# The output transfers of a streaming recurrent-memory kernel, issued by GpSimd in place of SyncE

## The chip, the cores and the metric

The kernel runs on one core of a Trainium2 chip. The metric is device time in microseconds. It was timed in three runs before the change: 2551.04, 2555.86 and 2556.03 us, median 2555.86 us. The profile is one further execution under the hardware profiler, 2564.14 us on the device, whose span from the first to the last instruction is 2562.2 us.

In the text PE is the matrix engine (TensorE), DVE the vector engine, ACT the scalar engine, POOL is GpSimd and SP is SyncE. "SPq" and "ACTq" in a row of the profile are the instruction queues of SP and ACT that issue transfers. L248 means line 248 of the kernel.

## The reference

The input x has 2048 rows of 1024 numbers in bfloat16. It is layer-normalised to xn, and the output is x + A(xn) + B(xn).

A is attention with a recurrent memory. The rows are cut into 64 segments of 32 rows. To each segment 8 memory rows are joined in front, so 40 rows are projected to queries, keys and values of 32 heads with 128 numbers each, attended under a mask, and projected back to 1024 columns. The first 8 of the 40 result rows are the memory of the next segment, so the segments must run one after another:

```
for s in range(n_seg):
    h = concatenate([mem, x[:, s*32:(s+1)*32]])        # 40 rows
    q, k, v = h @ Wq, h @ Wk, h @ Wv                   # 1024 -> 32 x 128, each
    o = softmax(mask(q k^T * scale)) v @ Wo            # 32 x 128 -> 1024
    mem = o[:, :8];  outs.append(o[:, 8:])
```

B scores all rows, takes the best two, puts them through a gated network with 3584 hidden numbers, scales them and adds them back at their two rows. It is done once, ahead of the segments.

## The kernel before

**Weights.** Wq, Wk, Wv and Wo together are 64 granules, each 128 partitions x 2048 numbers, 512 KB. 42 granules stay in SBUF for the whole kernel. The other 22 are read from HBM again in each of the 64 segments, through 6 slots (`wstream`, tile name `g`). `fetch` (L236 to L249) issues the next such transfer on SP at L248. `used(g)` calls it when the program has come past a streamed granule, so each fetch goes into the slot of the granule just used and has to wait until PE is done with it. The streamed granules are spread evenly, about one in three: 1, 4, 7, 10, 13 and so on.

**A segment.** Segment s has the place j = s mod 4 in its group of four, G. Six phases of 8 granules project the segment's rows (L507 to L534, matmuls at L510): Wq, Wk for the first half of the heads, Wq, Wk for the second, Wv, Wv. Rows that do not depend on the memory ("left" rows, 8 of each segment, four segments together) ride along in some phases (L514): in segments with j = 1 and j = 2 their queries and keys are made and written to DRAM (`qkl_d<-QS`, 128 KB, issued by ACT, twice in such a segment). Then 16 granules of Wo (L549) make the result WO. ACT and DVE cast it into OB (L575, L576), PE transposes OB, and DVE puts the 8 memory rows into the ST of the next segment (L267). With j = 3 the left rows of the group are projected as well, into WL and then OL (L591).

**Hooks.** Work beside the matmuls is hung on (phase, granule in the phase) by `hook` and run in the program after that granule. What matters here:

- (0, 2) of the next segment: `store`, four transfers of OB to the output on SP (L579), 24 rows of 512 B each, 12 KB.
- (0, 5) of the segment after a group's last: `store_left`, four transfers of OL on SP (L596), 32 rows of 512 B each, 16 KB.
- (1, 4): ACT issues the load ZT (L394); (2, 3): ACT issues the load of the next ST (L260).
- (2, 5) and (4, 5): `scores`. It begins with a POOL copy of the left keys from QKL into KT (L432), without which the score matmuls (L436, L438) can't run. `scores(0)` also clears a part of PL on POOL (L456).
- (4, 6): `split_z`, a copy and a clear on POOL (L398, L399).

After the last segment both stores are run at once.

**Queues.** Each engine takes its instructions in the program's order, and one that waits holds what is behind it. SP's queue holds the weight fetches and the stores; ACT's holds its computing and the loads ZT, ST, QKL, STL and the writes `qkl_d<-QS`; POOL's holds only the small operations named above.

**Landing counters.** The library that builds the program tells the landing of a transfer by a semaphore. The transfers of SP and ACT, in one common order, take eight such counters in turn. Where a counter comes round again, the new transfer is made to wait until the earlier transfer with this counter, eight places before it in that order, has landed, whatever either of them carries. In the program before, the four stores and the four left stores take places in this order like any other. Around the store of a segment with j = 3 the order is: load ZT, two fetches, load ST, four stores, then the fetch that follows the use of granule 4. This fetch is the eighth place after ZT. GpSimd's transfers have eight counters of their own, and none was issued before.

Of the kernel before, what the change touches and what calls it, by code (L numbers as in the profile page):

```python
# [25 lines left out]
def kernel(  # L26
# [16 lines left out]
    nc = tc.nc  # L43
# [4 lines left out]
    SEG = int(A_seg_len)  # L48
# [8 lines left out]
    XM = SEG - M  # L57
# [4 lines left out]
    out2 = out[0]  # L62
# [267 lines left out]
    for c in range(2):  # L330
        nc.sync.dma_start(out=zT_d[bass.ds(vals[c] >> 5, 1), :, :, bass.ds(vals[c] & 31, 1)].rearrange("s p k r -> p (s k) r"),
                          in_=ZNEW[:, :, c:c + 1])
# [38 lines left out]
    for s in range(NSEG):  # L371
# [131 lines left out]
        for p, (mat, half) in enumerate(PHASES):  # L503
            PSm = psA.tile([P, 512], F32, tag="acc", name="PSm")
            PSl = psL.tile([P, 512], F32, tag="accl", name="PSl") if mat in left else None
            for kc in range(KC):
                g = 8 * p + kc  # L507
# [68 lines left out]
        nc.vector.tensor_copy(out=OB[:, P:256], in_=WO[:, P:256])  # L576
        def store(OB=OB, s=s):
            for g in range(4):
                nc.sync.dma_start(out=out2[s * SEG:s * SEG + XM, 256 * g:256 * (g + 1)],  # L579
                                  in_=OB[32 * g:32 * g + XM, :])  # L580

        todo = [store]
# [6 lines left out]
        if j == 3:  # L589
            OL = one.tile([P, 256], BF16, tag="pm", name="OL")  # L590
            nc.scalar.copy(out=OL[:, :], in_=WL[:, 0:256])  # L591

            def store_left(OL=OL, G=G):
                o4 = out2[4 * G * SEG:4 * (G + 1) * SEG, :].rearrange("(s r) d -> s r d", s=4)
                for g in range(4):
                    nc.sync.dma_start(out=o4[:, XM:SEG, 256 * g:256 * (g + 1)], in_=OL[32 * g:32 * (g + 1), :])  # L596
            todo.append(store_left)
        if s + 1 < NSEG:
            ST = nxt["st"]
# [37 lines left out]
```

## Time and profile before

| | |
|---|---|
| median of three runs (lowest, highest) | 2555.86 us (2551.04, 2556.03) |
| profiled execution: on the device, its span | 2564.14 us, 2562.2 us |
| PE busy | 1865.3 us, 73% of the span |
| DVE, ACT, POOL busy | 638.4, 513.5, 108.0 us |
| moved by the DMA engines | 831.71 MB, of it 800.19 MB on SP's queue |
| mean granted clock of PE | 0.883 |
| first store issued | 237.1 us after the span's start |
| transfers of OB and OL | 256 and 64 |

The page's slices show for each fortieth of the span how many tenths an engine was busy, and the mean share of the 16 DMA engines that had a packet in work. "DMA share" in a table by stretches is the same share; as it is summed from packets, it can come out a little over 1. "A <- B: t, n, m" in a table of waits means that A waited t us in n waits, the longest m, and that B ended them. The chain of waits goes back from the end, at each step to what released it.

### The profile page before, as it was taken

The numbers are of one execution on the slowest core, as the hardware profiler recorded it, in microseconds if no ns is written. First come the engines' busy times: TensorE is split into PE (matmuls) and PEld (weight loads), VectorE is DVE, ScalarE is ACT, GpSimd is POOL, SyncE is SP. The second block draws the span as 40 slices with busy tenths as digits, with TensorE's granted clock in tenths as the row PEclk, the third lists the DMA queues.
The fourth block names the chain that finished last, engine by engine and source line by source line (L and its number), as shares of the span: only waits on it lengthen the run. The fifth ranks groups of instructions, "written<-read, shape, count | busy, mean of one in ns | idle before, by whom it ended". The sixth has DMA issues, their size and how long they took to land.

```text
span 2562.2 us, 82489 instructions
## 1 busy us (share of the span) xinstructions
PE 1865.3 (73%) x36873; PEld 975.1 (38%) x36873; DVE 638.4 (25%) x1733; ACT 513.5 (20%) x1145; POOL 108.0 (4%) x371
## 2 busy tenths in 40 slices
PE   4366777777777777677777777777776877777676
PEld 3233343344334334333433343343333433343333
DVE  5302222222222222222222222222232222222222
ACT  4202122121212212111221212122121221122111
POOL 4200000000000000000000000000000000000000
PEclk9568989898989989988898988999899988889889
DMA  9997999999999989989998999999998998999898
GB/s 333 298 353 244 341 320 323 316 351 340 311 332 326 340 297 328 335 299 334 329 349 302 344 322 321 341 330 339 313 334 309 360 320 302 334 327 340 320 336 293
DMA packets 368855, 831.71 MB, mean 325 GB/s; under 512 B 69458, under 2 KB 122738, under 8 KB 368500
## 3 DMA queue, kind: packets, MB, share of 16 engines
q1 hardware_dynamic: 303668, 800.19, 87.3%
q10 hardware_dynamic: 64832, 26.25, 3.8%
q8 instruction: 288, 4.72, 0.7%
q14 instruction: 67, 0.55, 0.1%
HBM read 804.28 MB, written 22.02 MB: 322 GB/s over the span
## 4 chain that ended last, share of the span: by engine, by line
DMA 62%; PE 27%; issue 4%; DVE 3%; ACT 2%; SPq 2%; ACTq 1%; POOL 0%; DVEq 0%; POOLq 0%
DMA g<-in_A_Wv_dram 15%; DMA g<-in_A_Wq_dram 14%; DMA g<-in_A_Wo_dram 13%; PE PSm L510 12%; DMA g<-in_A_Wk_dram 6%; PE WO L549 4%; PE PSl L514 3%; DMA qkl_d<-QS 2%; DMA QKL<-qkl_d 2%; PE WL L549 2%; DMA ZT<-zT_d 2%; PE PTq L408 1%; DMA ST<-xT_d 1%; SPq L248 1%; DMA zT_d<-Tz 1%
## 5 line engine op out<-in xcount | busy, mean ns | idle before, releaser
L510 PE MATMUL PSm<-wres,ST 128*32 128x512 bf16 x8192 | 785.2, 423 | 15.7 <-DVE ST L267 13.6
L510 PE MATMUL PSm<-g,ST 128*32 128x512 bf16 x4096 | 450.9, 427 | 325.8 <-DMA g<-in_A_Wk_dram 136.0
L510 PEld LDWEIGHTS <-ST 128*32 128x32 bf16 x12288 | 329.0, 101 | 770.2 <-issue 413.8
L549 PEld LDWEIGHTS <-OT 128*32 128x32 bf16 x8192 | 224.8, 102 | 170.5 <-issue 150.9
L522 ACT CAST XB<-PSm 128x512 bf16<-128x512 f32 x256 | 150.2, 587 | 660.6 <-PE PSm L510 535.2
L549 PE MATMUL WO<-wres,OT 128*32 128x256 bf16 x5120 | 248.2, 293 | 17.3 <-issue 17.3
L549 PE MATMUL WO<-g,OT 128*32 128x256 bf16 x3072 | 169.1, 294 | 99.6 <-DMA g<-in_A_Wo_dram 83.8
L514 PE MATMUL PSl<-wres,STL 128*32 128x512 bf16 x2048 | 210.4, 398 | 2.7 <-DMA STL<-stl_d 2.7
L488 ACT CAST OT<-OP 128x256 bf16<-128x256 f32 x256 | 95.5, 373 | 324.6 <-PE OP L485 324.6
L448 ACT ACTIVATE SPS<-SPS 128x320 f32<-128x320 f32 x128 | 54.0, 422 | 528.4 <-DVE SPS L447 503.7
L416 DVE COPY KT<-PTq 128x512 bf16<-128x512 bf16 x128 | 54.4, 425 | 348.9 <-PE PTq L408 348.6
L408 PE MATMUL PTq<-IDENT,XB 128*128 128x128 bf16 x1024 | 112.9, 240 | 35.6 <-ACT XB L522 33.6
L446 DVE TENSOR_REDUCE NM<-SPS 128x8 f32<-128x320 f32 x128 | 63.0, 492 | 302.0 <-PE SPS L441 302.0
L432 POOL COPY KT<-QKL 128x128 bf16<-128x128 bf16 x128 | 37.3, 291 | 2335.4 <-PE WO L549 1057.4
L490 DVE CAST OTL<-OP 128x64 bf16<-128x64 f32 x128 | 28.8, 225 | 406.8 <-ACT OT L488 406.8
L408 PEld LDWEIGHTS <-XB 128*128 128x128 bf16 x1024 | 64.2, 104 | 166.2 <-ACT XB L522 131.5
L413 DVE COPY QT<-PTq 128x512 bf16<-128x512 bf16 x128 | 53.2, 416 | 261.1 <-PE PTq L408 261.0
L514 PEld LDWEIGHTS <-STL 128*32 128x32 bf16 x3072 | 86.3, 100 | 70.8 <-issue 14.0
L483 PE MATMUL OP<-PT,VM 32*128 32x40 bf16 x2048 | 94.9, 180 | 19.3 <-ACT VM L532 14.4
L514 PE MATMUL PSl<-g,STL 128*32 128x512 bf16 x1024 | 105.2, 397 | 0.0
L483 PEld LDWEIGHTS <-VM 32*128 32x128 bf16 x2048 | 66.2, 92 | 94.9 <-issue 58.7
L485 PE MATMUL OP<-PT,VL 32*128 32x40 bf16 x2048 | 88.1, 176 | 4.2 <-ACT VL L534 4.2
(99 smaller groups left out, 1513.4 us busy)
## 6 DMA issues: line engine op xcount, KB each, us to landing
g<-in_A_Wq_dram SPq DMA_DIRECT2D x384, 512.0 KB
g<-in_A_Wo_dram SPq DMA_DIRECT2D x384, 512.0 KB
g<-in_A_Wk_dram SPq DMA_DIRECT2D x320, 512.0 KB
g<-in_A_Wv_dram SPq DMA_DIRECT2D x320, 512.0 KB
qkl_d<-QS ACTq DMA_DIRECT2D x64, 128.0 KB
QKL<-qkl_d ACTq DMA_DIRECT2D x128, 64.0 KB
g<-in_B_w_gate_dram SPq DMA_DIRECT2D x16, 448.0 KB
g<-in_B_w_up_dram SPq DMA_DIRECT2D x16, 448.0 KB
```

The source lines that it names most:

```text
L408: nc.tensor.transpose(out=PTq[:, il, :, :].rearrange("p j r -> p (j r)"), in_=XB[:, il * P:(il + 1) * P], identity=IDENT[:, :])
L413: nc.vector.tensor_copy(out=QT[half][:, :, :], in_=pv)
L416: nc.vector.tensor_copy(out=KT[half][:, :, 0:32], in_=pv)
L446: nc.vector.tensor_reduce(out=NM[:, :], in_=S8, axis=AX.X, op=ALU.max, negate=True)
L448: nc.scalar.activation(out=S8, in_=S8, func=ACTF.Exp, scale=SCALE)
L483: nc.tensor.matmul(o, lhsT=VM[half][q0:q0 + 32, il * P:(il + 1) * P], rhs=PTm[q0:q0 + 32, il, 0:NK], start=True, stop=False, tile_position ...
L485: nc.tensor.matmul(o, lhsT=VL[q0:q0 + 32, c0:c0 + P], rhs=PTl[q0:q0 + 32, il, 0:NK], start=False, stop=True, tile_position=(q0, 0), skip_g ...
L488: nc.scalar.copy(out=OT[half][:, 2 * ph:2 * ph + 2, :, :], in_=ov[:, :, :, 0:SEG])
L510: nc.tensor.matmul(PSm[32 * jq:32 * jq + 32, :], lhsT=ST[:, kc, :], rhs=Gv[:, 512 * jq:512 * (jq + 1)], start=(kc == 0), stop=(kc == KC - ...
L514: nc.tensor.matmul(PSl[32 * jq:32 * jq + 32, :], lhsT=STL[:, kc, :], rhs=Gv[:, 512 * jq:512 * (jq + 1)], start=(kc == 0), stop=(kc == KC - 1),
L522: nc.scalar.copy(out=XB[:, :], in_=PSm[:, :])
L549: nc.tensor.matmul(PS[32 * g:32 * g + 32, 0:256], lhsT=lhs(h), rhs=Gv[:, D * hs + 256 * g:D * hs + 256 * (g + 1)], start=False, stop=(last ...
```

## The change

The two places where the output is written (L579 and L596) now name GpSimd as the issuing engine. Their data, shapes, order and place in the program stay.

```diff
         def store(OB=OB, s=s):
             for g in range(4):
-                nc.sync.dma_start(out=out2[s * SEG:s * SEG + XM, 256 * g:256 * (g + 1)],
+                nc.gpsimd.dma_start(out=out2[s * SEG:s * SEG + XM, 256 * g:256 * (g + 1)],
                                   in_=OB[32 * g:32 * g + XM, :])
...
             def store_left(OL=OL, G=G):
                 o4 = out2[4 * G * SEG:4 * (G + 1) * SEG, :].rearrange("(s r) d -> s r d", s=4)
                 for g in range(4):
-                    nc.sync.dma_start(out=o4[:, XM:SEG, 256 * g:256 * (g + 1)], in_=OL[32 * g:32 * (g + 1), :])
+                    nc.gpsimd.dma_start(out=o4[:, XM:SEG, 256 * g:256 * (g + 1)], in_=OL[32 * g:32 * (g + 1), :])
```

A transfer issued by GpSimd has its descriptors written by software on that engine; one issued by SyncE or ScalarE has them made by hardware.

## The prediction

> **What bounds the kernel now.** I read the page first, then the waits of PE, then the waits of SP, then the stretches behind the stores. The page (span, DMA slices, DMA queue of SP):
>
> ```profile
> span 2562.2 us, 82489 instructions
> ...
> DMA  9997999999999989989998999999998998999898
> ...
> q1 hardware_dynamic: 303668, 800.19, 87.3%
> ```
>
> SP's queue, nearly all of it weights, keeps the DMA engines busy for most of the time, but not for all of it. PE's two largest waits are for these weights, us in total, number, longest:
>
> ```profile
> PE PSm L510 <- DMA g<-in_A_Wk_dram: 136.0, 93, 5.7
> PE PSm L510 <- DMA g<-in_A_Wq_dram: 99.9, 109, 4.1
> ```
>
> So the streamed weights set the pace. The DMA share (the next to last number) says whether the stream itself is full. Here is the whole stretch of the segments, one 12 us stretch late in a segment, and then the 9 us that begin 3 us after the first store transfer of eight segments in a row, with j = 1, 2, 3, 0, 1, 2, 3, 0:
>
> ```profile
> 237.00:2555.00 2318.00, 1744.98 (x35222) 897.58 (x35218) 569.35 (x1571) 455.54 (x1050) 63.29 (x313) 0.90 0.92 328
> 1150.00:1162.00 12.00, 9.27 (x242) 5.45 (x241) 3.42 (x11) 3.58 (x10) 0.27 (x2) 0.94 1.05 390
> 1129.00:1138.00 9.00, 7.60 (x149) 3.34 (x141) 2.83 (x6) 2.37 (x5) 0.29 (x1) 1.00 0.72 217
> 1167.00:1176.00 9.00, 7.62 (x145) 3.41 (x138) 3.78 (x11) 2.18 (x4) 0.62 (x3) 1.00 0.90 283
> 1203.00:1212.00 9.00, 4.88 (x85) 1.75 (x80) 1.42 (x3) 0.59 (x1) 0.62 (x3) 0.85 0.72 230
> 1243.00:1252.00 9.00, 5.00 (x89) 1.70 (x81) 3.03 (x9) 1.60 (x3) 0.62 (x3) 0.72 0.69 211
> 1278.00:1287.00 9.00, 6.32 (x129) 2.90 (x121) 3.30 (x10) 2.18 (x4) 0.62 (x3) 1.00 0.87 263
> 1312.00:1321.00 9.00, 7.32 (x141) 3.35 (x133) 3.66 (x10) 2.18 (x4) 0.62 (x3) 1.00 0.84 266
> 1348.00:1357.00 9.00, 4.87 (x93) 1.86 (x85) 1.81 (x4) 0.59 (x1) 0.62 (x3) 0.95 0.70 216
> 1388.00:1397.00 9.00, 4.51 (x97) 2.04 (x95) 3.77 (x10) 1.60 (x3) 0.62 (x3) 1.00 0.48 140
> ```
>
> Late in a segment the DMA engines are full (1.05, 390 GB/s). Behind every store there is a hole. With j = 3 it is this one: SP issues four stores, then nothing until 1206.50; a slice of that time moves 0 GB/s; and the chain of waits leads into the fetch at 1206.50 from the load of ZT, which lands at 1201.29 + 5.14 = 1206.43:
>
> ```profile
> 1199.84 3.77 SPq L579 DMA_DIRECT2D out_dram<-OB  x4
> 1206.50 0.36 SPq L248 DMA_DIRECT2D g<-in_A_Wq_dram  x1
> ```
> ```profile
> 1206.00:1207.00 1.00, 0.77 (x12) 0.27 (x12) 0.06 (x1) 0.00 (x0) 0.00 (x0) 1.00 0.00 0
> ```
> ```profile
> 1201.29 5.14 DMA ZT<-zT_d
> ```
>
> The fetch does not read ZT. It has ZT's landing counter, because four stores stand between them. The same in SP's waits over the whole span: stores that wait for weights and ZT, which they do not touch, and fetches that wait for ZT and QS:
>
> ```profile
> SPq L248 <- DMA qkl_d<-QS: 174.6, 48, 8.8
> SPq L248 <- DMA ZT<-zT_d: 57.2, 26, 3.5
> SPq L579 <- DMA g<-in_A_Wk_dram: 66.3, 61, 3.5
> SPq L579 <- DMA g<-in_A_Wq_dram: 10.6, 19, 1.1
> SPq L596 <- DMA g<-in_A_Wq_dram: 18.1, 15, 2.3
> SPq L596 <- DMA ZT<-zT_d: 10.6, 7, 3.6
> ```
>
> **The change part by part.** *Taken from SP:* 320 issues, and with them four or eight places in the turn of eight counters. SP's own issue time is off the path, since SP mostly waits; what counts is that fetches no longer stand behind stores. With j = 3 the place eight after ZT then falls on a QKL load, and the fetches after granules 4, 7 and 10 have their slots free as soon as PE is done with them. Six slots stay in use, so I expect the hole gone there. With j = 0 the same holds for eight stores in place of four. With j = 1 and 2 the writes of QS still share counters with fetches (the 174.6 us stay as they are, no store stands between them), and I take half of these holes as gone.
>
> From the eight rows, 9 us times (1 - share): j = 1 and 2: 2.52 + 0.90 + 1.17 + 1.44 = 6.03 us; j = 3 and 0: 2.52 + 2.79 + 2.70 + 4.68 = 12.69 us. Gone: half of the first and all of the second, 15.7 us in eight segments, 1.96 us in one. 63 segments follow a store: **124 us**. The unknown is how much of a filled hole comes back elsewhere. From below: nothing is gained, if other transfers hold the fetches as long. From above: the DMA engines are never idle, 2318 us times (1 - 0.92) = 185 us. I take 124 because the holes at j = 3 and 0 end with a wait that the change removes, and the stretches without stores are full.
>
> By the Trainium skill (DMA: Bandwidth & Descriptors, section "Issuing engines are not separate DMA queues") transfers of all engines run on the same 16 DMA engines, and issuing from another engine saves only the issue time, usually small; by that sentence alone the 124 us would be 0, while the rows above show fetches held by landings and not by issue time.
>
> *Given to POOL:* the issue of 4 or 8 transfers, ahead of the copy L432 in its queue. No row has a software-made transfer. The nearest rows are SP's issues of the same transfers (min, median, max in ns) and, for the longest that POOL takes over one instruction, an addition in the prologue (mean 2118 ns):
>
> ```profile
> L579 SPq DMA_DIRECT2D out_dram<-OB x256: 302/352/1460, 237.1 to 2556.8; - x128
> L596 SPq DMA_DIRECT2D out_dram<-OL x64: 615/618/773, 352.2 to 2559.3; - x64
> L168 POOL TENSOR_TENSOR XP<-XP,XN 128x1024 bf16<-128x1024 bf16 x16 | 33.9, 2118 | 42.2 <-ACT XN L163 42.2
> ```
>
> I bound it by 0.35 and 2.12 us and take 1.0 us, nearer to SP's issues, since these are the same transfers, than to a long POOL computation. What is queued behind: L432 (0.29 us), and behind it the score matmuls. The sources of the stores, that copy, and PE around its need of it:
>
> ```profile
> 1197.89 0.29 DVE L576 CAST OB<-WO 128x128 bf16<-128x128 f32 x1 [2.07 <-DMA g<-in_A_Wq_dram]
> ...
> 1234.97 0.29 DVE L576 CAST OB<-WO 128x128 bf16<-128x128 f32 x1 [2.19 <-ACT OB L575]
> ```
> ```profile
> 1239.38 0.37 ACT L591 CAST OL<-WL 128x256 bf16<-128x256 f32 x1 [4.44 <-PE WL L549]
> ```
> ```profile
> 1197.68 0.29 POOL L432 COPY KT<-QKL 128x128 bf16<-128x128 bf16 x1 [24.40 <-PE WO L549]
> ```
> ```profile
> 1209.60 0.62 PE L510 MATMUL PSm<-g,ST 128*32 128x512 bf16 x4 [2.83 <-DMA g<-in_A_Wq_dram]
> 1209.98 0.27 PE L436 MATMUL SPS<-KT,QT 128*32 128x40 bf16 x4
> ```
> ```profile
> 1247.44 0.62 PE L510 MATMUL PSm<-g,ST 128*32 128x512 bf16 x4 [2.04 <-DMA g<-in_A_Wq_dram]
> 1247.82 0.27 PE L436 MATMUL SPS<-KT,QT 128*32 128x40 bf16 x4
> ```
>
> At 1.0 us: OB is ready at 1198.18, four issues end at 1202.2, L432 at 1202.5; needed at 1209.98, or without PE's stall of 2.83 us at 1207.1. Hidden by the phases 0 and 1, 4.6 us to spare. With j = 0: OL is ready at 1239.75, the OB issues are done by then, four more end at 1243.75, L432 at 1244.0; needed at 1247.82 - 2.04 = 1245.8, 1.8 us to spare. Cost 0. At 0.35 us also 0. At 2.12 us the ordinary segment still just fits (1206.9 against 1207.1); with j = 0, where OB is ready at 1235.26, eight issues and L432 end at 1235.26 + 16.96 + 0.29 = 1252.5, 6.7 us late, 15 times: 101 us. Stores that are held longer free OB and OL later, but OB is written again a segment later, and OL's buffer (that of PM) only after these scores.
>
> *The end:* the last stores have no cover. The sources and SP's last issues:
>
> ```profile
> 2554.22 0.29 DVE L576 CAST OB<-WO 128x128 bf16<-128x128 f32 x1 [2.19 <-ACT OB L575]
> ```
> ```profile
> 2556.37 0.37 ACT L591 CAST OL<-WL 128x256 bf16<-128x256 f32 x1 [2.18 <-PE WL L549]
> ```
> ```profile
> 2557.31 2.63 SPq L596 DMA_DIRECT2D out_dram<-OL  x4
> ```
>
> SP's last issue ends at 2559.94, and 2.26 us later the span ends. On POOL eight issues of 1.0 us from 2554.51 end at 2562.5, so **+2.6 us** (at 0.35 us -1.8, at 2.12 us +11.5).
>
> *Sum:* the profiled execution's 2564.1 - 124 + 2.6 = 2442.7 us. It lies 8.3 us over the median of the runs (2555.86), so for the median: **2434 us**.
>
> **The rivals.** *Half the gain* (A): the fetches meet the next landing in turn, QS, QKL or ST, and the holes move. For it: the 174.6 us behind QS and the holes of 0.90 and 0.84 where QS is written. Against it: only j = 1 and 2 write QS. 62 us less: 2496 us.
>
> *No change* (B): the holes come from the slots, not from the counters; SP would have waited for PE anyway, as it does elsewhere, and POOL's stores only save issue time. For it: in a stream with a fixed number of slots a late fetch often just follows a late PE. Against it: the chain goes through a landing at 1206.43, not through PE, and PE itself then waited 2.83 us for weights. 2556 us. This is also what the skill's sentence above gives.
>
> *Slower* (C): POOL's software descriptors take so long that L432 is late and PE waits at the scores, in each segment. With p us for an issue the ordinary segment is late by 4p - 8.7 (1198.18 + 4p + 0.29 against 1207.15), that with j = 0 by 8p - 10.2 (1235.26 + 8p + 0.29 against 1245.78). The change loses from 48(4p - 8.7) + 15(8p - 10.2) = 124, p = 2.2 us. At 2.5 us, four times SP's 0.62, the two terms are 62 + 147 = 209 us, and the end (2554.51 + 20 against 2559.94) is 15 us later: 2556 - 124 + 209 + 15 = 2656 us. For it: nothing in the trace limits p. Against it: POOL's longest instruction takes 2.12 us for 128 x 1024 elements, a transfer has 24 or 32 rows.
>
> The Trainium skill (SBUF — State Buffer, the box "The 'DVE blocks DMA' trap (SWDGE)") says that software descriptors cannot be written while DVE copies in a mode that uses both ports. It asks for operands in SBUF; the DVE copies behind the stores (L576 above, from WO) read PSUM, so by the rule it would add nothing here.
>
> *More* (D): full DMA engines, 2564 - 185 - 8 = 2371 us.
>
> **How the numbers follow.** The forecast, 2390 to 2470 us, has 0.58; A 0.14; B 0.09; C 0.13; D 0.06. Faster by over 0.2% (what a measurement here can tell from no change) are forecast, A and D: 0.78; same B: 0.09; slower C: 0.13. The range leaves out C and about half of D: it goes from D's 2371, rounded down to 2370, to 2561, the upper end of B's 0.2%. Within it the forecast's own 2390 to 2470 allows the 124 us to be 88 to 168.
>
> **What would show it.** Right: no fetch waits for ZT; in the nine microseconds behind a store with j = 3 or 0 the DMA share is over 0.9; PE's waits for Wk and Wq fall to about half; L432 starts 5 us later and no score matmul waits for it. Wrong: SP's waits at L248 for QS, ST or QKL grow by as much as those at L579 and L596 vanish (A); the hole stays with SP waiting for PE (B); PE waits for POOL's L432 (C).

## The result and the profile after

The changed kernel takes 2371.85 us (median of four runs, 2369.39 to 2383.86) against 2555.95 us for the kernel before (2551.04 to 2559.93): a ratio of 0.929, 95% interval 0.9255 to 0.9325, or 184 us less. The profiled execution took 2369.39 us. The forecast was 2434 us, so the way was right; the gain was forecast at two thirds of what came (122 of 184 us).

The page of the changed kernel (span, DMA slices, queues of SP and of GpSimd):

```profile
span 2367.6 us, 82555 instructions
...
DMA  9996999999999999999999999999999999999997
...
q1 hardware_dynamic: 292148, 795.98, 92.0%
...
q0 software_dynamic: 10240, 4.25, 0.7%
```

The stores are on a queue of their own now, and the slices with 8 tenths that the kernel before showed all along the segments are gone. The stretches, as in the prediction: first all segments, then 9 us from 3 us after the first store of eight segments in a row (j = 1, 2, 3, 0, twice). The last two numbers are DMA share and GB/s. The stores begin 0.3 us after OB is ready (median over the segments), against 2.0 us before, because they no longer stand behind a fetch.

```profile
237.00:2360.00 2123.00, 1648.56 (x35158) 876.16 (x35150) 565.26 (x1569) 453.05 (x1048) 229.30 (x629) 0.95 0.99 356
1036.00:1045.00 9.00, 6.99 (x84) 2.71 (x80) 1.54 (x3) 1.75 (x3) 0.00 (x0) 0.81 1.02 370
1073.00:1082.00 9.00, 7.73 (x149) 3.56 (x141) 2.68 (x6) 1.78 (x5) 0.62 (x3) 1.00 0.89 311
1109.00:1118.00 9.00, 5.18 (x105) 2.23 (x105) 3.33 (x10) 1.59 (x3) 0.62 (x3) 1.00 1.03 404
1139.00:1148.00 9.00, 6.45 (x88) 2.58 (x84) 0.56 (x2) 1.48 (x3) 2.79 (x6) 0.81 0.96 328
1172.00:1181.00 9.00, 7.25 (x96) 2.86 (x92) 1.54 (x3) 1.75 (x3) 0.00 (x0) 0.83 1.02 377
1207.00:1216.00 9.00, 8.92 (x161) 4.11 (x157) 2.23 (x5) 1.76 (x3) 0.62 (x3) 0.91 0.90 341
1242.00:1251.00 9.00, 7.20 (x133) 2.94 (x129) 2.88 (x8) 2.18 (x4) 0.68 (x3) 0.95 0.98 341
1277.00:1286.00 9.00, 6.79 (x125) 3.24 (x120) 1.64 (x4) 1.17 (x2) 3.03 (x8) 0.88 0.96 331
```

Over the segments the share went from 0.92 to 0.99 and the rate from 328 to 356 GB/s. In these eight stretches the mean rate is 350 GB/s against 228 before (2803 and 1826, divided by eight), and in these rows the holes are closed at all four places j. Over all 63 segments that follow a store, the same nine microseconds carry 346 GB/s on average, against 227 before; only with j = 0 they stay low (282, before 186). Outside these stretches the rate is the same in both kernels: taking them out of the two rows for all segments leaves 361 GB/s before and 360 now. So the whole gain lies behind the stores. PE's waits for the weights of the phases behind the store, 136.0 (Wk) and 99.9 us (Wq) before, are now:

```profile
PE PSm L510 <- DMA g<-in_A_Wq_dram: 51.2, 103, 2.1
PE PSm L510 <- DMA g<-in_A_Wk_dram: 27.5, 48, 1.8
```

What SP waits for at its fetches in the changed kernel:

```profile
SPq L248 <- DMA QKL<-qkl_d: 119.9, 67, 5.0
SPq L248 <- DMA ZT<-zT_d: 117.6, 42, 5.3
...
SPq L248 <- DMA qkl_d<-QS: 114.6, 44, 6.6
...
SPq L248 <- DMA ST<-xT_d: 91.5, 32, 5.3
```

and two of the same rows of the kernel before, which the prediction did not show:

```profile
SPq L248 <- DMA QKL<-qkl_d: 136.7, 60, 5.1
...
SPq L248 <- DMA ST<-xT_d: 9.8, 13, 2.2
```

So the waits for other engines' transfers did not go away. Those for ZT and ST grew by 142 us together, while those for QS (174.6 us in the prediction's rows) and QKL fell by 77. The fetches still share eight counters with ACT's transfers.

GpSimd's side, the groups of its transfers (count, busy us, mean ns) and a segment with j = 0:

```profile
L579 POOL DMA_DIRECT2D out_dram<-OB x256 | 129.1, 511 | 1374.5 <-DVE OB L576 1346.1 <-issue 28.4
L596 POOL DMA_DIRECT2D out_dram<-OL x64 | 38.3, 606 | 24.5 <-ACT OL L591 24.5
```
```profile
1136.40 1.99 POOL L579 DMA_DIRECT2D out_dram<-OB  x4 [21.38 <-DVE OB L576]
1139.60 2.40 POOL L596 DMA_DIRECT2D out_dram<-OL  x4 [1.20 <-ACT OL L591]
1141.99 0.30 POOL L432 COPY KT<-QKL 128x128 bf16<-128x128 bf16 x1
```

An issue takes 0.51 or 0.61 us of GpSimd. The copy L432 begins 5.6 us after the first store, and the score matmuls wait for it twice in the whole span, as before (10.7 us in two waits then):

```profile
PE SPS L436 <- POOL KT L432: 12.2, 2, 7.7
```

The end became longer. The last work of GpSimd in the changed kernel, and the drains of GpSimd at the program's end (min, median, max in ns), changed kernel first, then the kernel before:

```profile
2357.99 2.40 POOL L596 DMA_DIRECT2D out_dram<-OL  x4
```
```profile
L632 POOLq DRAIN  x3: 34/107/7302, 2359.5 to 2367.4; - x3
```
```profile
L632 POOLq DRAIN  x3: 34/82/236, 2531.4 to 2562.0; - x3
```

The last issue ends at 2360.39. SP has seen all landings by 2362.3, but the span ends at 2367.6, behind a drain of 7.3 us that took 0.24 us before.

### The profile page after: what moved, and what is told of

Same layout as the page of the kernel before. It is cut to its first block, busy times and chain, and to the rows that moved or that the text cites. A ratio compares the mean times of both kernels' runs of the same rounds, so it can differ in the third digit from the quotient of the medians.

```text
span 2367.6 us, 82555 instructions
## 1 busy us (share of the span) xinstructions
PE 1775.0 (75%) x36873; PEld 955.7 (40%) x36873; DVE 635.5 (27%) x1733; ACT 512.1 (22%) x1145; POOL 276.4 (12%) x691
## 4 chain that ended last, share of the span: by engine, by line
DMA 60%; PE 26%; DVE 5%; issue 3%; ACT 3%; ACTq 1%; SPq 0%; POOL 0%; POOLq 0%; DVEq 0%
DMA g<-in_A_Wo_dram 19%; DMA g<-in_A_Wv_dram 15%; PE PSm L510 11%; DMA g<-in_A_Wq_dram 9%; PE WO L549 5%; DMA g<-in_A_Wk_dram 4%; DMA ST<-xT_d 3%; PE PSl L514 3%; DMA qkl_d<-QS 2%; PE WL L549 2%; DMA zT_d<-Tz 2%; PE PTq L408 1%; DMA QKL<-qkl_d 1%; DMA ZT<-zT_d 1%; ACT XB L522 1%
## 5 line engine op out<-in xcount | busy, mean ns | idle before, releaser
L510 PE MATMUL PSm<-wres,ST 128*32 128x512 bf16 x8192 | 736.0, 398 | 19.9 <-DVE ST L267 13.6
L510 PE MATMUL PSm<-g,ST 128*32 128x512 bf16 x4096 | 421.1, 398 | 163.4 <-DMA g<-in_A_Wv_dram 79.2
L510 PEld LDWEIGHTS <-ST 128*32 128x32 bf16 x12288 | 317.9, 98 | 558.0 <-issue 271.4
L579 POOL DMA_DIRECT2D out_dram<-OB x256 | 129.1, 511 | 1374.5 <-DVE OB L576 1346.1
L514 PE MATMUL PSl<-wres,STL 128*32 128x512 bf16 x2048 | 205.0, 388 | 3.0 <-DMA STL<-stl_d 3.0
L408 PE MATMUL PTq<-IDENT,XB 128*128 128x128 bf16 x1024 | 104.1, 226 | 88.8 <-ACT XB L522 86.5
L408 PEld LDWEIGHTS <-XB 128*128 128x128 bf16 x1024 | 59.2, 99 | 211.0 <-ACT XB L522 194.8
L432 POOL COPY KT<-QKL 128x128 bf16<-128x128 bf16 x128 | 37.8, 296 | 569.0 <-PE SPS L438 354.4
```

The lines of the kernel that those rows point to most:

```text
L408: nc.tensor.transpose(out=PTq[:, il, :, :].rearrange("p j r -> p (j r)"), in_=XB[:, il * P:(il + 1) * P], identity=IDENT[:, :])
L510: nc.tensor.matmul(PSm[32 * jq:32 * jq + 32, :], lhsT=ST[:, kc, :], rhs=Gv[:, 512 * jq:512 * (jq + 1)], start=(kc == 0), stop=(kc == KC - ...
L514: nc.tensor.matmul(PSl[32 * jq:32 * jq + 32, :], lhsT=STL[:, kc, :], rhs=Gv[:, 512 * jq:512 * (jq + 1)], start=(kc == 0), stop=(kc == KC - 1),
L579: nc.gpsimd.dma_start(out=out2[s * SEG:s * SEG + XM, 256 * g:256 * (g + 1)], in_=OB[32 * g:32 * g + XM, :])
```

## The experiments

The theory under test: the stores cost time by the places that they take in the turn of the eight landing counters, so that stores and fetches wait for transfers that they have nothing to do with. The first rival: it is the stores' bytes, writes or issue in SP's queue. Later runs ask whether what is left in the changed kernel is of the same kind. Each ratio is against the kernel before, timed beside the run on the same chip. The medians of the kernel before lie between 2556 and 2562 us on all of them, so the times of different rows are compared as they stand.

| run | median us | ratio, 95% interval |
|---|---|---|
| changed kernel | 2371.85 | 0.929 (0.9255 to 0.9325) |
| e1_places4 | 2618.42 | 1.0241 (1.0175 to 1.0307) |
| e1_places2 | 2491.04 | 0.9737 (0.9676 to 0.9799) |
| e2_one_place | 2409.66 | 0.942 (0.9359 to 0.948) |
| e3_act | 2442.08 | 0.9536 (0.9473 to 0.9598) |
| e4_ob_only | 2421.57 | 0.9462 (0.9428 to 0.9496) |
| e5_loads_pool | 2282.73 | 0.8919 (0.8892 to 0.8945) |
| e6_res43 | 2335.99 | 0.9111 (0.9079 to 0.9143) |
| e7_before43 | 2463.4 | 0.9635 (0.9591 to 0.9679) |
| e10_loads_pool43 | 2331.16 | 0.9147 (0.9074 to 0.9219) |
| e12_loads_places | 2420.86 | 0.9465 (0.9408 to 0.9522) |
| e13_all_pool43 | 2353.12 | 0.9189 (0.9134 to 0.9245) |
| e14_spread | 2561.93 | 1.002 (0.9986 to 1.0054) |

### Places without the output: e1_places4 and e1_places2

To the changed kernel, behind GpSimd's stores:

```diff
+            for g in range(4):          # 2 in e1_places2
+                nc.sync.dma_start(out=dum_d[0, s, g:g + 1, :], in_=x2[0:1, 0:64])
...
+                for g in range(4):      # 2 in e1_places2; with the left stores
+                    nc.sync.dma_start(out=dum_d[1, G, g:g + 1, :], in_=x2[0:1, 0:64])
```

> The stores stay on GpSimd. Where SP issued them before, it now issues four (and four for the left stores) copies of 128 bytes from x to a scratch place in DRAM that nobody reads: they only take places in the turn of the eight landing counters. If the places are the cause (theory), fetches again wait for ZT and for weights, the holes behind the stores come back and the time is 2530 to 2575 us, near the kernel before. If it is the output's bytes, or its writes, in SP's queue (rival), the time stays at 2372 to 2395 us.

> As the run with four, with two such 128-byte copies at each of the two places. Theory: fewer places reach back less far into the weights and ACT's loads, part of the holes comes back: 2400 to 2520 us. Rival: 2372 to 2385 us.

Measured: 2618 and 2491 us. With none, two and four foreign places the time is 2372, 2491 and 2618 us, though the output's bytes stay out of SP's queue. The rival's bytes and writes are out: with four copies the nine microseconds behind the 63 stores carry 220 GB/s, as in the kernel before (227). SP's waits in e1_places4 (its L583 and L601 are the new copies, L249 the fetch):

```profile
SPq L583 <- DMA g<-in_A_Wk_dram: 57.4, 56, 3.2
...
SPq L601 <- DMA ZT<-zT_d: 22.9, 13, 3.0
...
SPq L583 <- DMA g<-in_A_Wq_dram: 11.6, 21, 1.2
```

A copy of 128 bytes that reads only x waits for weights and for ZT, as the stores did. The time is 43 us over the range's upper end and 2.4% over the kernel before.

These two runs alone do not exclude the third part of the rival, the time that SP spends on issuing. The copies need it too: 0.58 us for one (median), 192 us in all, against 138 us for the stores in the kernel before. That may be a part of what the copies cost beyond the stores; it was not separated. SP's timeline gives a bound. Of the 78 fetches in e1_places4 that come directly behind copies, 45 still waited after the last copy, so its issue did not hold them. Before the other 33, the issues of copies since SP's last wait sum to 66 us, of the 247 us that this run lies over the changed kernel. The same count in the kernel before gives 32 fetches and 60 us, of the 184 us. So issuing can be a part of the gain by this count, but not most of it. The runs e3_act and e12_loads_places below take places without any issue on SP.

### All the bytes in one place: e2_one_place

```diff
-            for g in range(4):
-                nc.sync.dma_start(out=out2[...], in_=OB[32 * g:32 * g + XM, :])
+            nc.sync.dma_start(out=scr_d[0, s, :, :], in_=OB[:, :])
...
-                for g in range(4):
-                    nc.sync.dma_start(out=o4[...], in_=OL[32 * g:32 * (g + 1), :])
+                nc.sync.dma_start(out=scr_d[1, G, :, :], in_=OL[:, :])
```

> The kernel before with the stores on SP, but each four stores are one transfer of the whole 128x256 block of OB (or OL) to a scratch place in DRAM: 64 KB in place of 48 KB, one place in place of four. The output is not written. Theory (places): most of the gain is there, 2375 to 2440 us. Rival (bytes or writes in SP's queue): 2540 to 2590 us, as before.

Measured: 2410 us, in the theory's range. This kernel leaves the output unwritten. For OB, SP writes a third more bytes than before (64 KB in place of 48 KB), and yet the gain is four fifths of the change's (5.8% of 7.1%). Behind the 63 stores the rate is 346 GB/s, as in the changed kernel. The run also takes away three quarters of the stores' issues on SP.

### Another queue with the same counters: e3_act

```diff
-                nc.gpsimd.dma_start(out=out2[...
+                nc.scalar.dma_start(out=out2[...
-                    nc.gpsimd.dma_start(out=o4[...
+                    nc.scalar.dma_start(out=o4[...
```

> The stores issued by ACT in place of GpSimd: SP's queue is as free as with GpSimd, but the stores take places in the same turn of eight counters, and ACT is held while they wait. Theory (places): the holes stay, 2520 us or more, above 2556 if ACT's own work is late. Rival (SP's queue held by the stores' issues and order): 2370 to 2420 us.

Measured: 2442 us, between the two. My theory as written expected 2520 us or more, so it was too simple. A place costs in two ways. The store itself waits for its counter and holds the queue that it stands in, and the transfer eight places later waits for it. On ACT the first falls on ACT and not on the fetches, as does the time for the issue; the second stays. The waits at SP's fetches, and then of ACT, in this run:

```profile
SPq L248 <- DMA out_dram<-OB: 134.8, 72, 5.3
```
```profile
ACT XB L522 <- DMA out_dram<-OB: 140.4, 32, 6.2
```

How the remaining 70 us over the changed kernel split between these two rows was not tried.

### One part alone: e4_ob_only

```diff
-                    nc.gpsimd.dma_start(out=o4[...
+                    nc.sync.dma_start(out=o4[...
```

> One part of the change alone: the stores of OB are issued by GpSimd, the left stores of OL by SP as before. Theory (places in the turn of counters): only one segment in four, that with j = 0, still has four foreign places, 15 times some 3 us: 2395 to 2440 us. If the parts do not add up (one of them carries all): 2372 or 2556 us.

Measured: 2422 us, in the range. The left stores, a fifth of the transfers, carry 50 us, 3.3 us for each of the 15 segments that they fall into; the stores of OB carry the rest. The left stores alone were not moved, so that the parts add up is not shown.

### Spread, not fewer: e14_spread

```diff
-        todo = [store]
+        todo = [lambda g=g, st=store: st(g) for g in range(4)]
...
-            hook(0, 2 + 3 * n, fn)
+            hook(*divmod(2 + 2 * n, 8), fn)
```

`store` and `store_left` issue one transfer each time, all on SP.

> The kernel before, all on SP, but the four stores (and four left stores) are not issued in one go: each hangs on its own granule, every second one from granule 2 on, so that one fetch stands between them or none. As many places as before. Theory in its sharper form (it is the run of foreign places between two fetches that empties the stream): 2420 to 2510 us. If the number of places in a segment is what counts: 2540 to 2570 us.

Measured: 2562 us, the same as before within 0.6%. The sharper form, that it needs a run of stores between two fetches, falls. With e1_places4 and e1_places2, it is the number of foreign places that counts. The stores wait no less when they stand singly: at the last two rows here (L578 is the store) 134 us, where the kernel before has 77 us.

```profile
SPq L248 <- DMA QKL<-qkl_d: 215.9, 81, 7.8
...
SPq L578 <- DMA g<-in_A_Wk_dram: 71.9, 63, 3.6
...
SPq L578 <- DMA g<-in_A_Wq_dram: 61.8, 37, 3.9
```

### The same for ACT's loads: e5_loads_pool and e12_loads_places

e5_loads_pool, to the changed kernel:

```diff
-        nc.scalar.dma_start(out=ST.rearrange("p k r -> p (k r)"), in_=xT_d[s // 4][s % 4])
+        nc.gpsimd.dma_start(out=ST.rearrange("p k r -> p (k r)"), in_=xT_d[s // 4][s % 4])
...
-        nc.scalar.dma_start(out=t[:, :, :], in_=qkl_d[...
+        nc.gpsimd.dma_start(out=t[:, :, :], in_=qkl_d[...
...
-            nc.scalar.dma_start(out=Zt[:, :, :], in_=zT_d[s])
+            nc.gpsimd.dma_start(out=Zt[:, :, :], in_=zT_d[s])
```

> The changed kernel, and also the loads ZT, ST and QKL are issued by GpSimd in place of ACT, so that no fetch shares a counter with them; only the writes of QS and the loads STL stay in SP's turn. In the changed kernel fetches wait 330 us for these three. If those waits still cost (holes that are left), 2300 to 2355 us. If the DMA engines are the bound now (share 0.99), the waits cost nothing: 2360 to 2380 us. If GpSimd is held by a load and is late with the left keys: over 2385 us.

e12_loads_places adds to this, behind each of the three:

```diff
+        nc.scalar.dma_start(out=dum_d[n:n + 1, :], in_=x2[0:1, 0:64])
```

> The kernel with stores and the loads ZT, ST and QKL on GpSimd (2283 us), and for each of these loads ACT issues a copy of 128 bytes to a scratch place in DRAM where it issued the load before: the places in the turn of counters are back, the bytes and the software descriptors stay as they were. Theory (the gain from 2372 to 2283 us came from the shared counters): 2345 to 2400 us. Rival (it came from GpSimd's larger and fewer packets, 322521 against 367576): 2283 to 2305 us.

Measured: 2283 us, 10.8% under the kernel before and better than I expected of it, and 2421 us with the places put back. So the waits for ZT, ST and QKL that were left in the changed kernel still cost time, and they cost it through the counters, since the copies bring almost no bytes and nothing is added to SP's queue. (ACT issues once more for each load, 0.50 us each; what that costs was not separated.) In e12_loads_places the fetches wait for the copies instead:

```profile
SPq L256 <- DMA dum_d<-in_A_x_dram: 252.1, 113, 5.1
```

It ends 49 us over the changed kernel, above my range; the tiny copies again cost more than the transfers whose places they hold, and why is open. The stretch of the segments in e5_loads_pool:

```profile
237.00:2270.00 2033.00, 1590.51 (x35178) 852.38 (x35177) 565.59 (x1569) 443.92 (x1049) 394.02 (x876) 0.98 1.00 372
```

The DMA share of the changed kernel was 0.99, yet the rate rises from 356 to 372 GB/s. The share near 1 did not mean that the stream was full.

### Bytes against depth: e6_res43, e7_before43, e10_loads_pool43, e13_all_pool43

```diff
-N_RES = 42
-N_SLOT = 6
+N_RES = 43
+N_SLOT = 5
```

on the changed kernel, on the kernel before, on e5_loads_pool, and in e13_all_pool43 on e5_loads_pool with L426 (writes of QS) and L351 (STL) issued by GpSimd too.

> The changed kernel with 43 resident granules and 5 slots in place of 42 and 6, the same SBUF: 21 granules streamed in a segment in place of 22, 33.6 MB less in all. If the DMA engines are the bound and five slots keep them full, the bytes at 356 GB/s give 94 us: 2275 to 2300 us. If the depth of the stream is what counts (fewer fetches in flight), 2372 us or more.

> The same trade (43 resident, 5 slots) in the kernel before, stores on SP. Theory: with five slots a fetch that is held by a counter empties the stream sooner, so the holes grow and eat a part of the 94 us: 2490 to 2580 us, against 2462 if the holes stayed as they are.

> Stores and loads ZT, ST, QKL on GpSimd, and 43 resident granules with 5 slots. If the DMA engines are the bound now, 33.6 MB less at 375 GB/s give 90 us: 2190 to 2215 us. If with five slots PE's own uneven pace leaves the stream empty at times, as the 36 us in place of 94 of the same trade in the changed kernel suggest: 2235 to 2265 us. If the depth counts for all: 2283 us or more.

> As the run before, and also the writes of QS and the loads STL on GpSimd: in the segments SP's counters serve weight fetches alone, and with five slots no fetch can wait for a counter. If QS's counters still cost: 15 to 40 us under the run before. If GpSimd, which is then held until ACT has QS ready, is late with the left keys or loads: 10 us or more over it. Else the same within 10 us.

Measured: 2336, 2463, 2331 and 2353 us. The trade gives the kernel before about the whole 94 us that the expectation puts on the bytes (2556 to 2463), against the theory's expectation. In its trace the holes did not grow: the nine microseconds behind the 63 stores carry 261 GB/s, against 227 without the trade. So they became shallower, and the 93 us are not the price of the bytes alone. It gives the changed kernel 36 of them, and e5_loads_pool loses 48 us by it (2283 to 2331). So neither the changed kernel nor e5_loads_pool is bound by the bytes alone. In e5_loads_pool, which has fewer false waits than the other two, the sixth slot is worth more than the bytes. The segments of e10_loads_pool43, and SP's longest wait in it (489.2 us in e5_loads_pool):

```profile
237.00:2320.00 2083.00, 1645.38 (x35284) 866.90 (x35284) 567.79 (x1573) 445.21 (x1051) 396.01 (x884) 0.95 0.97 349
```
```profile
SPq L248 <- PE PSm L510: 589.4, 701, 4.5
```

SP waits longer for PE to free a slot and the rate is 349 GB/s, against 372 with six slots. With QS and STL on GpSimd too, no landing of another engine can hold a fetch in the segments, and nothing is gained: the median is 22 us higher, with intervals that overlap. In the trace of e13_all_pool43 GpSimd waits 454.5 us for ACT's QS, and the left keys come late for the score matmuls, 59.7 us against 8.7 in e10_loads_pool43. That this is what the 22 us are made of was not tested.

```profile
PE SPS L436 <- POOL KT L432: 59.7, 33, 5.2
```

The fastest of the kernels tried is e5_loads_pool, 2282.73 us.

## Why the prediction was right, point by point

**The cause** was right. Fetches and stores were held by landings through shared counters (e1_places4, e1_places2, e2_one_place), also where SP issues nothing more (e3_act, e12_loads_places). Against the prediction's sentence that SP's own issue time is off the path, up to some 60 us of the gain can be issuing. Of the signs, PE's waits for Wk and Wq fell even to a third, and the DMA share with j = 3 and 0 is over 0.9 in the rows shown; over all 15 segments with j = 0 its mean is 0.88. The reading of the single hole, ZT's landing at 1206.43 and the fetch at 1206.50, was the key to it. That the holes come from a *run* of stores was part of how I told it, and e14_spread shows it wrong.

**The 124 us** are the term that was mis-sized. It failed in two steps. I measured the holes by DMA share, 9 us times (1 - share), 2.34 us in a segment. By bytes the same rows say more: at 228 GB/s against the 350 GB/s that these stretches reach now, 9 us times (1 - 228/350) = 3.1 us, in 63 segments 198 us; with the rates of all 63 stretches, 227 and 346 GB/s, it is 195 us. In the holes of these eight rows the engines still count as busy for 0.74 of the time, at 228 GB/s. And I took only half of the holes at j = 1 and 2 as gone, because of QS; by bytes they went from 257 to 350 GB/s in these rows and closed like the others. The waits for QS fell from 174.6 to 114.6 us, which I had held constant because no store stood between. With j = 1 that was misread: in the program's order the segment's first write of QS is followed by a store, ZT, a store, a fetch, ST and three fetches, so two stores stand between the write and the fetch eight places behind it. 198 us less 4.5 at the end is near the 194.8 by which the profiled execution became shorter (2564.14 to 2369.39). This sum uses the rate that came out, which the prediction did not have.

**The upper bound** was no bound. I took 185 us as what never-idle DMA engines would give (D, 2371 us), and the time came out there. But e5_loads_pool is 88 us under it with the same bytes and a share of 1.00. That D's number was met is chance: the changed kernel still has waits that cost. The time lies below the forecast's own 2390 to 2470 us and 2 us above the lower end of the wide range, 2370 us, which is this bound rounded down. That it did not fall below it is luck too.

**GpSimd's cost** of 1.0 us for an issue was 0.51 and 0.61 us, and the conclusion that L432 is hidden holds. C needed 2.2 us. The Trainium skill's trap of DVE and software descriptors (SBUF — State Buffer, the box "The 'DVE blocks DMA' trap (SWDGE)") did not show: median and largest issue of a store of OB were 0.51 and 0.71 us.

**The end** was to cost 2.6 us. From OL ready to the span's end it takes 9.9 us (2357.7 to 2367.6) against 5.5 us (2556.74 to 2562.2), so 4.5 us more. With 0.5 us an issue the stores alone would have ended sooner than I thought; the drain of 7.3 us, which I did not foresee, is the difference.

**The rivals.** A was right in kind: false waits moved to ZT and ST (142 us more), contrary to my sign "no fetch waits for ZT". By its own measure A failed: the waits for ST, QS and QKL together grew by 5 us, while the 106 us at the stores vanished. The waits that are left cost less than the holes that went; without those for ZT, ST and QKL e5_loads_pool is 89 us faster. B is refuted, and with it the sentence of the Trainium skill (DMA: Bandwidth & Descriptors, "Issuing engines are not separate DMA queues") that another engine saves only issue time: in this kernel, where the program ties the transfers of two queues together by counters, it saved 184 us, of which SP's issue time can hold some 60 by the count above.

## What to carry to other kernels

When a transfer or its queue waits for the landing of something that it does not read, look for a shared completion counter, and count how many transfers use the turn between two prefetches. Here it paid to take small transfers that need no speed out of the turn that the prefetch stream uses, by fewer and larger transfers (e2_one_place) or by an engine with counters of its own; that engine was GpSimd, which was busy for 12% of the span in the changed kernel. Measure a hole in a stream by its bytes and not by the share of busy DMA engines.

## What the runs showed that I had not expected

- A software-made store of 12 KB takes GpSimd 0.51 us, of 16 KB 0.61 us. SP's issues of the same took 0.35 and 0.62 us.
- In the changed kernel GpSimd's drain at the program's end takes 7.3 us, in e5_loads_pool 9.2 us, against 0.24 us in the kernel before and in e3_act, which have no software-made transfers (one execution of each). The span ends only behind it.
- DMA share does not tell a full stream: 0.99 at 356 GB/s in the changed kernel, 1.00 at 372 GB/s in e5_loads_pool.
- PE's granted clock rose with the stream, 0.883 to 0.938 in the profiled executions, and 0.954 in e5_loads_pool. That PE's fewer pauses are the reason was not tested. The clock does not show in the time between runs of one kernel: e2_one_place took 2409.34 us at 0.923 and 2409.98 us at 0.948.
